# Two layers of linear attention and gated MLP on one core: nine zero products ahead of the first turn, first loads on either queue, turns in transpose mode, a new split of the last tile and a new order

## The chip, the cores and the metric

The kernel runs on one core of a Trainium2 chip. The metric is device time in microseconds (us) of one execution. Five engines matter: PE (TensorE, matrix products), DVE (VectorE), ACT (ScalarE), POOL (GpSimd) and SP (SyncE, which here does nothing but issue transfers). PE loads weights in parallel with products (PEld). Transfers are issued by SP, and a few by ACT, and run on 16 DMA engines.

## The reference

The input x is 2048 rows of 512 in bf16. Two layers run one after the other, each made of an attention block A and an MLP block B, with the same weights in both layers:

```python
q, k, v = split(layernorm(x) @ wqkv)          # 32 heads of 16
phi(u) = [softmax(u @ w_phi), softmax(-u @ w_phi)]   # per head, 16 + 16 wide
kv = phi(k).T @ v ;  z = sum over rows of phi(k)     # per head, over all 2048 rows
x = x + ((phi(q) @ kv) / (phi(q) @ z + 1e-6)) @ wo
n = layernorm(x)
x = x + ((relu(n @ W_gate) * (n @ W_up)) @ W_down)   # 1376 wide inside
```

The sums kv and z run over all rows. So no row of a layer's attention output can be made before the keys and values of all rows of that layer are done.

## The kernel before

The 2048 rows are 16 tiles of 128. A tile passes these steps in a layer, each a numbered operation ("op") of one engine:

- normalise (L479 to L506): row statistics on DVE (`stats` L481, 0.60 us, and `aggr` L482), `ln` and `rstd` on ACT (L489, L491), scaling on DVE (`xnA` L499).
- turn: the normalised 128x512 tile is transposed, as the products need the 512 on the partitions. Most tiles go by a DMA transpose on SP's queue, two tiles at a time (L465). The first four tiles of layer 0, the last two of layer 1's keys, and a few tiles in the MLP and in front of `wo` are turned by PE: four products with an identity matrix into a PSUM bank of 512 fp32 columns (L470), then a copy to SBUF (`evac`, L428 to L432) on ACT or DVE.
- keys and values: `K` (L539) and `V` (L545), each four products of 512 columns. ACT takes exp of the key product with both signs (`ek`, two of 512 columns), DVE sums over 16 (`sk` L550), ACT makes the reciprocal (`lnk`, `rk`), POOL or DVE scales (`phi` L513, two halves a tile), and PE adds the tile to the sums (`kvz` L574, eight products of 65 columns).
- queries: `Q` (L601), exp (`Eq`), sum (`sq` L607), scaling (`rat`, `phq` on POOL or DVE), then a DMA transpose (`fq` L627).
- When all 16 `kvz` are done, DVE writes the summed matrix into `R` (L586). Then `erq` (L638), division, `o`, turn, `proj` with `wo` (L661), residual, and the MLP: `G` and `Up` (L738), ReLU and product, `down` (L778), residual (`resB` L785). The MLP goes in blocks of 1 to 4 tiles.

The key and query weights are folded with w_phi at the start: the key weight `wk` is turned by PE (`turn` L444, four ops m = 0 to 3 of four products), copied (`wT`), multiplied by a block-diagonal `Wblk` (`fold` L452, ops 0 to 3), and copied to `Wk` (`W2`). `K` of any tile needs all four `W2`. The query weight takes the same way with DMA transposes (`wT` L439) and folds 4 to 7. Below, fold 4 to 7 and W2 4 to 7 are those of the query weight.

Which engine does an op and when is written down by hand-over tables. `PLACE` is a string of 0 and 1, one for each op that two engines can do; 1 takes the other engine. `SLOTS` gives each buffer its place in its pool. `ORDER` lists all 1880 ops in one sequence; each engine executes its own ops in that sequence, in order, and waits at an op until its inputs are there. So a wait on an engine holds all that stands behind it. `IDLE` puts so many products with a zero matrix ahead of the n-th PE op; before the first one PE does eight of them (L425), which only keep PE busy.

Transfers take turns on eight completion semaphores: a load waits in its queue until the load eight places earlier has landed. First loads before: ACT issues `x` of tile 0 and half of `wk` (row blocks 2 and 3 of four, "wk2"); SP issues `wf`, the other half ("wk0", which turns 0 and 1 read; turns 2 and 3 read wk2), `x` of tiles 1, 2, 3, 4-5, 12-13, and then the first DMA transpose of the query weight.

Of the kernel before, what the change touches and what calls it, by code (L numbers as in the profile page):

```python
# [8 lines left out]
P = 128  # L9
D = 512  # L10
# [3 lines left out]
NB = D // P  # L14
# [128 lines left out]
class K:  # L143
# [9 lines left out]
    "0101010100000000001100000001110000101110000110101000000100000101000000010000100000011000000011101010"  # L153
    "1010011010111000101011000001100011100001011100000101101000111000000011000111010011000001101100001011"
    "0110101011100110011100010111110101000100110000001000001100000111100100010000110001001001011010111001"
    "010000101101110101001101111111110"
)
SLOTS = (
    "0011432021055021001401501045313321124221352412451013e0315g31303b0305c12201i012432332391030654220f321"
    "4h220030344d100111082247052a331k1615010b1250052c1344300g0132252j045e363d1200040401141402000224011020"  # L160
    "0400001134021012100000203101002122001002541105001002511102104910002413114215400412511651100100120031"
    "1420302310051535031h432112311505010425412301310405420324310022031410j5100a24022k02327101200410401103"
    "12242250121002352020511310154521505223522020e4231c031213111011021411125513140225000g3420030030020120"
    "03413125121121433231f0121f214i00181651332422193104055j333k204b360a2243033d242h304i113805010401021210"
    "0000121002100010010021140010123402000043001010020111302020011511301002431321101003205504010521311411"
    "5402110501523540013000121032150140030110232043213110025124210401311015522400200403422412313320414041"
    "210100300531330452512524210005215103213300111020141500412"
)
IDLE = (
    0, 0, 0, 1, 0, 0, 0, 0, 0, 0, 1, 0, 1, 0,  # L170
# [101 lines left out]
)  # L272


# [620 lines left out]
```

## Time and profile before

| what | value |
|---|---|
| median of 3 runs | 375.89 us (375.27 to 376.62) |
| the profiled execution | 376.44 us, of which the span (first to last instruction) 374.7 us |
| PE busy in the span | 363.8 us (97%) |
| DVE, ACT, POOL busy | 275.9, 204.3, 80.4 us |
| first product of `K` | 10.18 us |
| first `erq` (all keys of layer 0 summed) | 56.30 us |
| last product starts / last store has landed | 371.22 / 373.71 us |

A row of the groups reads: line, engine, operation, output<-inputs, shape and count, then busy time and mean duration, then the idle time of the engine ahead of these instructions and what ended it. A row of the stages reads: stretch, length, then busy us and count of PE, PEld, DVE, ACT and POOL, the granted clock, the DMA share and GB/s. Durations are longer than what an instruction holds its engine, as neighbours overlap; where the text counts a queue it takes the distance from start to start of neighbours without a wait: 0.863 us for four products of 512 columns, 0.26 for `kvz`, 0.223 for four of 128 columns, 0.477 for an ACT exp of 512, 0.465 for an ACT copy of 512, 1.129 for `sk` and `sq`, 0.60 for `stats`, 0.602 for `phi` on DVE, 1.014 on POOL, 0.60 for a DVE copy of 512 out of PSUM, 0.335 for a DVE product of 512 bf16 from SBUF.

### The profile page before, as it was taken

What the parts mean: (1) busy time and instruction counts of PE and PEld (TensorE: products, weight loads), DVE (VectorE), ACT (ScalarE), POOL (GpSimd) and SP (SyncE); (2) the same over time, 40 slices, a digit from 0 to 9 for tenths busy, and PEclk for the clock granted to TensorE, in tenths of its full rate; (3) what the DMA queues carried; (4) which work ended last, traced back from release to release, by engine and by line L of the source; (5) the groups of instructions that cost most, each with busy time, mean ns of one, the idle gap of its engine ahead of it and who ended that gap; (6) DMA issues with size and microseconds to landing.
All of it is one profiled execution on the core that took longest, in us unless ns stands there. A gap on an engine that the chain in (4) does not pass through costs nothing.

```text
span 374.7 us, 7403 instructions
## 1 busy us (share of the span) xinstructions
PE 363.8 (97%) x2784; PEld 216.1 (58%) x2830; DVE 275.9 (74%) x587; ACT 204.3 (55%) x561; POOL 80.4 (21%) x93
## 2 busy tenths in 40 slices
PE   7998999999999999999999999999999999999996
PEld 3453455867544544466566456587764444457674
DVE  6999999998775956864789989998776365134333
ACT  5998999655545546344539666874434423313111
POOL 0286985430101100110033533241100000000000
PEclk9999999999999999999999999999999999999999
DMA  8997439875532233042212100488753302020221
GB/s 233 204 232 195 131 81 175 142 142 112 96 59 54 44 65 63 1 84 52 42 38 48 36 0 3 85 115 121 147 94 79 57 0 58 0 56 2 69 74 42
DMA packets 93443, 31.20 MB, mean 83 GB/s; under 512 B 85248, under 2 KB 92384, under 8 KB 93408
## 3 DMA queue, kind: packets, MB, share of 16 engines
q1 hardware_dynamic: 92992, 30.34, 40.1%
q8 instruction: 22, 0.36, 0.4%
q10 hardware_dynamic: 416, 0.39, 0.4%
q14 instruction: 13, 0.11, 0.1%
HBM read 7.91 MB, written 2.10 MB: 27 GB/s over the span
## 4 chain that ended last, share of the span: by engine, by line
PE 89%; issue 1%; ACT 0%; DVE 0%; DVEq 0%
PE b L738 37%; PE b L778 20%; PE b L661 7%; PE b L601 6%; PE b L545 6%; PE b L539 5%; PE b L714 3%; PE q L638 2%; PE q L574 2%; PE b L470 1%; ACT ek L604 0%; DVE o L652 0%; DVE X L785 0%; DVEq L890 0%; ACT lnA L489 0%
## 5 line engine op out<-in xcount | busy, mean ns | idle before, releaser
L738 PE MATMUL b<-xnTB,wgu 128*128 128x128 bf16 (+2 forms) x1200 | 154.5, 279 | 0.2 <-ACT rd L649 0.2
L738 PEld LDWEIGHTS <-wgu 128*128 128x128 bf16 x1200 | 97.5, 98 | 47.3 <-DMA xnTB<-xn 0.4
L742 ACT ACTIVATE gu<-b 128x512 bf16<-128x512 f32 (+1 forms) x83 | 47.2, 581 | 84.8 <-PE b L738 82.0
L778 PE MATMUL b<-wd,hT 128*128 128x512 bf16 (+2 forms) x342 | 83.9, 372 | 0.9
L513 POOL TENSOR_TENSOR ek<-ek,sk 128x512 bf16<-128x512 bf16 x43 | 46.7, 1107 | 122.6 <-ACT sk L562 121.7
L778 PEld LDWEIGHTS <-hT 128*128 128x128 bf16 (+1 forms) x363 | 34.7, 98 | 34.2 <-DVE hT L746 0.2
L755 DVE TENSOR_TENSOR hT<-gu,b 128x512 bf16<-128x512 bf16 (+1 forms) x47 | 30.8, 666 | 30.2 <-ACT gu L742 16.4
L607 DVE TENSOR_REDUCE sq<-ek 128x64 f32<-128x1024 bf16 x32 | 38.4, 1210 | 3.6 <-ACT ek L604 3.5
L604 ACT ACTIVATE ek<-b 128x512 bf16<-128x512 f32 x64 | 37.0, 606 | 6.9 <-PE b L601 6.7
L542 ACT ACTIVATE ek<-b 128x512 bf16<-128x512 f32 x64 | 36.8, 623 | 6.6 <-PE b L539 6.6
L550 DVE TENSOR_REDUCE sk<-ek 128x64 f32<-128x1024 bf16 x32 | 38.2, 1205 | 1.8 <-ACT ek L542 1.8
L785 DVE SCALAR_TENSOR_TENSOR X<-b,rsB,X 128x512 bf16<-128x512 f32 (+1 forms) x33 | 23.9, 729 | 21.2 <-PE b L778 21.0
L757 ACT CAST gu<-b 128x512 bf16<-128x512 f32 (+1 forms) x36 | 20.5, 569 | 25.9 <-PE b L738 25.7
L539 PE MATMUL b<-Wk,xnTA 128*128 128x512 bf16 x122 | 32.2, 379 | 1.1 <-DMA xnTA<-xn 0.6
L545 PE MATMUL b<-wv,xnTA 128*128 128x512 bf16 x124 | 31.8, 379 | 1.3 <-ACT ek L604 1.0
L661 PE MATMUL b<-wo,oT 128*128 128x512 bf16 x121 | 31.5, 379 | 0.4
L622 POOL TENSOR_TENSOR ek<-ek,sq 128x512 bf16<-128x512 bf16 x24 | 25.3, 1060 | 30.4 <-DVE rsB L701 14.3
L601 PE MATMUL b<-Wq,xnTA 128*128 128x512 bf16 x121 | 30.8, 379 | 0.4
L665 DVE SCALAR_TENSOR_TENSOR X<-b,X 128x512 bf16<-128x512 f32 x32 | 22.0, 686 | 9.8 <-PE b L661 9.4
L652 DVE TENSOR_TENSOR o<-q,rd 128x512 bf16<-128x512 f32 x32 | 22.0, 687 | 2.8 <-PE b L738 1.2
L481 DVE BATCH_NORM_STATS2 bstA<-X 128x6 f32<-128x512 bf16 x32 | 21.1, 681 | 2.0 <-DMA X<-in_A_x_dram 1.8
L746 DVE TENSOR_TENSOR hT<-gu 128x512 bf16<-128x512 bf16 (+1 forms) x36 | 15.2, 424 | 10.1 <-ACT gu L757 10.0
(74 smaller groups left out, 351.0 us busy)
## 6 DMA issues: line engine op xcount, KB each, us to landing
out_dram<-X SPq DMA_DIRECT2D x15, 128.0 KB, 1.8
X<-in_A_x_dram SPq DMA_DIRECT2D x6, 256.0 KB, 4.5
wgu<-in_B_W_up_dram SPq DMA_DIRECT2D x4, 344.0 KB, 3.5
wgu<-in_B_W_gate_dram SPq DMA_DIRECT2D x4, 344.0 KB, 4.7
wd<-in_B_W_down_dram SPq DMA_DIRECT2D x5, 256.0 KB, 3.4
wv<-in_A_wqkv_dram SPq DMA_DIRECT2D x2, 256.0 KB, 4.4
wo<-in_A_wo_dram SPq DMA_DIRECT2D x4, 128.0 KB, 3.5
fq<-ek SPq DMA_TRANSPOSE x32, 3.3
```

Source lines behind the costliest of these rows:

```text
L513: e.tensor_tensor(out=out().rearrange("p g s (h f) -> p (g s h) f", f=DH)[:, lo:lo + n], in0=ek.t[:].rearrange("p g s (h f) -> p (g s h) f ...
L539: k = op("PE", mm(4, 512), due, lambda: [nc.tensor.matmul(kp.t[:], lhsT=xnTA[c][:, i, b, :], rhs=Wk2[:, b, :], start=(b == 0), stop=(b == ...
L542: e = [op("ACT", act(512), due, lambda s=s: nc.scalar.activation(out=ek.t[:, :, s, :], in_=kp.t[:].rearrange("p (g e) -> p g e", e=GQ), fu ...
L545: v = op("PE", mm(4, 512), due_v, lambda: [nc.tensor.matmul(vp.t[:], lhsT=xnTA[c][:, i, b, :], rhs=wv[:, b, :], start=(b == 0), stop=(b == ...
L550: a = op("DVE", SUM16, due, lambda: nc.vector.tensor_reduce(out=sk.t[:, row, :], in_=ek.t[:].rearrange("p g s (h f) -> p (g s h) f", f=DH) ...
L601: q = op("PE", mm(4, 512), due, lambda: [nc.tensor.matmul(qp.t[:], lhsT=xnTA[c][:, i, b, :], rhs=Wq2[:, b, :], start=(b == 0), stop=(b == ...
L604: e = [op("ACT", act(512), due, lambda s=s: nc.scalar.activation(out=ek.t[:, :, s, :], in_=qp.t[:].rearrange("p (g e) -> p g e", e=GQ), fu ...
L607: a = op("DVE", SUM16, due, lambda: nc.vector.tensor_reduce(out=sq.t[:], in_=ek.t[:].rearrange("p g s (h f) -> p (g s h) f", f=DH), axis=A ...
L661: a = op("PE", mm(4, 512), due + 3, lambda j=j, yp=yp: [nc.tensor.matmul(yp.t[:], lhsT=oT.t[:, j, b, :], rhs=wo[:, b, :], start=(b == 0), ...
L738: nc.tensor.matmul(ps.t[:, q * W:(q + 1) * W].rearrange("p (i t) -> p i t", t=P), lhsT=wgu[:, s, b, g * P:(g + 1) * P], rhs=xT.t[:, 0:n, b ...
L742: nc.scalar.activation(out=gu.t[:, 0, 0:cols], in_=gp.t[:, 0:cols], func=AF.Relu)
L778: nc.tensor.matmul(yp.t[:, 0:c1 - c0], lhsT=h.t[:m, f * W + i * P:f * W + (i + 1) * P], rhs=wd[:m, f, c0:c1], start=(f == 0), stop=(f == N ...
```

## The change

- The op ahead of the first turn makes nine zero products instead of eight. `IDLE` holds two products ahead of fold 4, instead of one each ahead of fold 0, fold 4 and the first `K`.
- The loads of `x` of tiles 0 and 1 and of the two halves of `wk` can be issued by SP or ACT, and `PLACE` has four more digits for them. They begin 1, 1, 0, 1: `x` of tile 0 and wk2 move to SP, `x` of tile 1 moves to ACT. So ACT issues one of these loads, and SP three.
- PE turns (`turn`, and the four-product turns of `xnTA`, `xnTB`, `oT`) use transpose mode. The result stands in bf16 in the first half of the PSUM bank, and the copies read bf16. The arrangement tables count a DVE copy of it at double rate.
- The last tile of layer 1 makes its output columns as 384 and 128 instead of 256 and 256.
- `ORDER`, `SLOTS` and `PLACE` are new throughout. PE's work is the same ops.

The diff without the tables:

```diff
-    op("PE", mm(8, 512), 0, lambda: idle(8), [c_z], [wps], name="warm")
+    op("PE", (3630, 3800, 9), 0, lambda: idle(9), [c_z], [wps], name="warm")
...
-    def load(due, dst, src, nbytes, eng="SP", follow=()):
-        q = nc.sync if eng == "SP" else nc.scalar
-        return op(eng, dma(nbytes), due, lambda: q.dma_start(out=dst, in_=src), name="load", follow=follow,
-                  move=nbytes / RATE)
+    def load(due, dst, src, nbytes, eng="SP", follow=(), both=False):
+        queues = {"SP": nc.sync, "ACT": nc.scalar}
+        ways = {e: (e, dma(nbytes), lambda q=q: q.dma_start(out=dst, in_=src), False) for e, q in queues.items()}
+        return op(eng, dma(nbytes), due, ways[eng][2], name="load", follow=follow, move=nbytes / RATE,
+                  alt=ways["ACT" if eng == "SP" else "SP"] if both else None)
...
+    def half(ps):
+        return ps.t[:].bitcast(BF16)[:, 0:NB * P]
...
-            tr = op("PE", mm(4, 128), due + m, lambda m=m, ps=ps: [nc.tensor.matmul(
-                ps.t[:, b * P:(b + 1) * P], lhsT=w[:, m, b * P:(b + 1) * P], rhs=ident[:], start=True, stop=True)
+            tr = op("PE", mm(4, 128), due + m, lambda m=m, ps=ps: [nc.tensor.transpose(
+                half(ps)[:, b * P:(b + 1) * P], w[:, m, b * P:(b + 1) * P], ident[:]) for b in range(NB)], ...
...
-            halves = ((0, 256), (256, 512)) if l == 1 and t == T - 1 else ((0, 512),)
+            halves = ((0, 384), (384, 512)) if l == 1 and t == T - 1 else ((0, 512),)
...
 IDLE = (
-    0, 0, 0, 1, 0, 0, 0, 0, 0, 0, 1, 0, 1, 0,
+    0, 0, 0, 0, 0, 0, 0, 0, 0, 0, 0, 2, 0,
 )
```

The tables read out by engine, for the first ops (numbers behind a name are tiles; `turn`, `fold`, `wT` and `W2` carry their own numbers; x12 stands for tiles 12-13, and so on):

| engine | before | after |
|---|---|---|
| SP | wf, wk0, x1, x2, x3, x4, x12, query turn 0, wv2, x8, wv0, x14, query turn 2, x6, query turn 1, wo, turn of tiles 4-5, W_down, turn of 12-13, W_down, x10, W_down, query turn 3, W_up, W_down, wo, W_gate, turn of 8-9 | wk0, x0, wf, wk2, x3, x12, x4, query turn 0, x2, wv2, wv0, query turn 3, x8, query turn 2, W_up, turn of 4-5, x6, query turn 1, x14, wo, W_down, turn of 8-9, wo, x10, turn of 12-13 |
| ACT | x0, table, wk2, ln and rstd 0, wT 0 and 1, ln 1, W2 0, rstd 1, wT 3, wT 2, copy of tile 0's turn, W2 1, 3, 2 | x1, table, ln and rstd 1, ln 0, wT 0 and 1, rstd 0, wT 2, W2 0, 1, 2, 3, copy of tile 1's turn |
| DVE | constants, masks, zero, stats 0, Wblk, stats 1, xnA 0, stats 2, 3, xnA 1 | zero, constants, masks, stats 1, stats 0, Mg, Wblk, xnA 1, xnA 0, wT 3, stats 3, copy of tile 0's turn |
| PE | 8 zero products, turns 0, 1, (1) fold 0, turns 3, 2, turn of tile 0, folds 1, 3, 2, (1) fold 4, turn of tile 1, (1) K0, K1 | 9 zero products, turns 0 to 3, folds 0, 1, turn of tile 1, fold 2, turn of tile 0, fold 3, (2) fold 4, K0, K1 |

Over the whole kernel `phi` on DVE goes from 21 to 15 (POOL 43 to 49), `phq` on DVE from 8 to 5, `vext` copies on DVE from 7 to 4, `ssq` on DVE from 11 to 15, the direct MLP product on DVE from 47 to 44, and six tiles turned by PE are copied by DVE instead of one, besides wT 3. Ahead of the first `R` DVE's queue loses one `sq`, one `vext` copy and one `phq`, and gains the copies wT 3 and of the turns of tiles 0 and 2, and one `rat`.

More of the change, by code (lines that the diff above doesn't have):

```diff
@@ L361, in w_load @@
     def w_load(w, k, b, eng):
-        return lambda f: load(b, w[:, b:b + 2, :], wqkv[:, b:b + 2, k * D:(k + 1) * D], 262144, eng, f)
+        return lambda f: load(b, w[:, b:b + 2, :], wqkv[:, b:b + 2, k * D:(k + 1) * D], 262144, eng, f, w is wk)
     def first_x(t, n, eng="SP"):
@@ L423, in idle, with evac @@
             nc.tensor.matmul(wps.t[:, 0:NB, :], lhsT=zero[:, 0:P], rhs=zero[:], start=True, stop=True)
-    op("PE", mm(8, 512), 0, lambda: idle(8), [c_z], [wps], name="warm")
-    def evac(eng, due, out_, in_, deps, takes, uses, name, cols=512):
+    op("PE", (3630, 3800, 9), 0, lambda: idle(9), [c_z], [wps], name="warm")
+    def evac(eng, due, out_, in_, deps, takes, uses, name, cols=512, rate=1):
         both = {"ACT": ("ACT", act(cols), lambda: nc.scalar.copy(out=out_(), in_=in_()), False),
-                "DVE": ("DVE", dve(cols), lambda: nc.vector.tensor_copy(out=out_(), in_=in_()), False)}
+                "DVE": ("DVE", dve(cols, rate), lambda: nc.vector.tensor_copy(out=out_(), in_=in_()), False)}
         _, cost, copy, _ = both[eng]
         return op(eng, cost, due, copy, deps, takes, uses, name=name, alt=both["DVE" if eng == "ACT" else "ACT"])
+    def half(ps):
+        return ps.t[:].bitcast(BF16)[:, 0:NB * P]
     def fold(w, dst, loaded, due, step, engs, by_dma=False):
@@ L443, in fold @@
             ps = Buf(p_b)
-            tr = op("PE", mm(4, 128), due + m, lambda m=m, ps=ps: [nc.tensor.matmul(
-                ps.t[:, b * P:(b + 1) * P], lhsT=w[:, m, b * P:(b + 1) * P], rhs=ident[:], start=True, stop=True)
-                for b in range(NB)], [loaded[m * len(loaded) // NB], c_id], [ps] + ([wT] if m == 0 else []),
+            tr = op("PE", mm(4, 128), due + m, lambda m=m, ps=ps: [nc.tensor.transpose(
+                half(ps)[:, b * P:(b + 1) * P], w[:, m, b * P:(b + 1) * P], ident[:]) for b in range(NB)], [loaded[m * len(loaded) // NB], c_id], [ps] + ([wT] if m == 0 else []),
                 [] if m == 0 else [wT], name="turn")
             turned.append(evac(engs[m % 2], due + m, lambda m=m: wT.t[:, :, m * P:(m + 1) * P],
-                               lambda ps=ps: ps.t[:].rearrange("p (b d) -> p b d", d=P), [tr], (), [ps, wT], "wT"))
+                               lambda ps=ps: half(ps).rearrange("p (b d) -> p b d", d=P), [tr], (), [ps, wT], "wT",
+                               rate=2))
         for m in range(NB):
@@ L469, in turn @@
         ps = Buf(p_b)
-        a = op("PE", mm(NB, 128), due, lambda: [nc.tensor.matmul(
-            ps.t[:, b * P:(b + 1) * P], lhsT=src.t[:, 0, b * P:(b + 1) * P], rhs=ident[:], start=True, stop=True)
-            for b in range(NB)], after + [c_id], [ps], [src], name=name)
-        return evac("ACT", due, lambda: dst()[:, 0], lambda: ps.t[:].rearrange("p (b t) -> p b t", b=NB), [a],
-                    takes, [ps] + uses, name, 512)
+        a = op("PE", mm(NB, 128), due, lambda: [nc.tensor.transpose(
+            half(ps)[:, b * P:(b + 1) * P], src.t[:, 0, b * P:(b + 1) * P], ident[:]) for b in range(NB)], after + [c_id], [ps], [src], name=name)
+        return evac("ACT", due, lambda: dst()[:, 0], lambda: half(ps).rearrange("p (b t) -> p b t", b=NB), [a],
+                    takes, [ps] + uses, name, 512, 2)
     def nothing():
```

28 lines of the change are left out of this document (14 added, 14 removed), and 180 rows, old and new, of the table ORDER.

## The prediction

> **What bounds the kernel now.** I read the totals and the chain that ended last first, then the stages, then PE's waits, then the timeline of the start and SP's queue.
>
> ```profile
> PE 363.8 (97%) x2784; PEld 216.1 (58%) x2830; DVE 275.9 (74%) x587; ACT 204.3 (55%) x561; POOL 80.4 (21%) x93
> ...
> PE 89%; issue 1%; ACT 0%; DVE 0%; DVEq 0%
> ```
>
> PE is busy 97% of the span, and the chain is PE's. The change leaves PE's products as they are (the turns keep their number and their 128 columns, 11 zero products stay 11), so time can only be won where PE waits: 374.7 - 363.8 = 10.9 us. The stages tell where.
>
> ```profile
> 0.00:40.00 40.00, 35.12 (x233) 17.55 (x238) 36.51 (x78) 33.40 (x96) 18.78 (x24) 1.00 0.88 208
> 40.00:80.00 40.00, 39.31 (x432) 25.62 (x437) 39.08 (x65) 34.46 (x109) 26.53 (x32) 1.00 0.66 135
> 80.00:120.00 40.00, 39.56 (x285) 23.95 (x288) 29.56 (x78) 21.17 (x60) 2.18 (x3) 1.00 0.50 92
> ...
> 360.00:374.70 14.70, 11.44 (x134) 8.78 (x131) 5.30 (x9) 1.95 (x4) 0.00 (x0) 1.00 0.16 49
> 20.00:40.00 20.00, 18.28 (x130) 9.11 (x131) 20.00 (x32) 17.82 (x53) 15.47 (x16) 1.00 0.85 207
> 40.00:56.00 16.00, 15.84 (x141) 8.65 (x143) 16.00 (x18) 15.72 (x48) 14.91 (x16) 1.00 0.40 109
> ```
>
> 4.9 us lie in the first 40, 3.3 in the last stage (the store and the end), and 2.7 in all between. The second thing to see is DVE's column: 20.00 of 20 and 16.00 of 16 up to the first `erq` at 56.30. There DVE has no hole at all, while PE has 1.7 + 0.2.
>
> ```profile
> PE q L423 <- DVE zero L394: 2.0, 1, 2.0
> PE b L545 <- ACT ek L604: 1.0, 1, 1.0
> PE b L452 <- ACT hT L429: 0.7, 2, 0.4
> PE b L539 <- DMA xnTA<-xn: 0.6, 1, 0.6
> PE b L539 <- ACT Wk L429: 0.2, 1, 0.2
> ```
>
> These are PE's waits of the first 40 us. The order of the start:
>
> ```profile
> 0.83 0.07 DVE L396 MEMSET vext<- 128x8 bf16 x1 [0.83 <-PEq L879]
> 1.63 0.27 DVE L394 MEMSET zero<- 128x256 uint32 x1
> 1.96 3.59 PE L423 MATMUL q<-zero 128*128 128x512 bf16 x8 [1.96 <-DVE zero L394]
> 5.57 0.82 PE L444 MATMUL b<-ident,hT 128*128 128x128 bf16 x8
> 6.20 1.07 ACT L429 CAST hT<-b 128x512 bf16<-128x512 f32 x2 [1.74 <-PE b L444]
> 9.35 1.61 ACT L429 CAST Wk<-b 128x512 bf16<-128x512 f32 x3
> 11.01 1.71 PE L539 MATMUL b<-Wk,xnTA 128*128 128x512 bf16 x6 [0.24 <-ACT Wk L429]
> ```
>
> From 6.20 on ACT copies without a hole; its last `Wk` copy ends at 10.96 and K0's third product starts at 11.01. PE's rate changes on the way: zero products start 0.427 apart, the turns 0.107 until 6.06, then 0.056, and later 512 columns take 0.216. The granted clock shows 1.00 in all these stages, so the step has to be read from the spacing; it came 4.1 us after PE's first product.
>
> **The change, part by part.**
>
> *Zero products.* `zero` becomes DVE's first op: 0.83 + 0.27 = 1.10, and PE follows 0.06 later as before, at 1.16. Nine at 0.427 end at 5.00. Before, eight ended at 5.34 and the first turn waited until 5.57 for wk0, which landed at 5.52.
>
> *First loads.* wk0 goes first on SP (0.74 instead of 1.25); with its old 4.28 it lands at 5.0, with fewer bytes ahead perhaps at 4. Turn 0 thus starts at 5.0, 0.57 earlier. wk2 becomes SP's fourth load. The five loads x0, x1, wf, wk0 and wk2 had all landed at 5.83 before, and are now the first five again, so I take 5.83 (bounds 5.3, as before, and 6.2, one tile's load later). The first query turn has 128 KB less ahead, so 8.57 or earlier. ACT's part falls from two issues to one (0.47).
>
> *ACT to K0.* Its first copy came 0.63 after the first turn's start: 5.63. Then wT 0, 1 (0.477 each), one `rstd` (0.10), wT 2, W2 0 to 3: seven copies, the last from 8.6 to 9.2. Before, ACT had wT 3, the copy of tile 0's turn, and two more small ops in this row, so 10.96 becomes 9.2. Wait of the inputs: turn 3 ends about 6.7 if PE is still slow, `fold` 0 by 6.95, W2 0 starts 7.16: hidden. wT 3 and tile 0's copy now wait in DVE's queue, which reaches them at 7.0 and 8.0, ahead of need. K0 ends about 9.5 instead of 11.4, and K1, behind ACT's copy for tile 1, starts at 9.75 instead of 11.68: PE is 1.9 us ahead.
>
> *What is late next: DVE.* PE's queue from K0 to the first `erq` holds 44 x 0.863 + 16 x 0.26 + 5 x 0.223 = 43.2 us in both orders. Before, 10.18 + 43.2 = 53.4 became 56.30, so 2.9 was lost on the way. With no wait at all it would now be about 8.6 + 43.2 = 51.8 (K0's end less its own 0.86). But `erq` needs `R`, and DVE's queue ahead of `R` shrinks only by `sq` 1.129 + `vext` 0.601 + `phq` 0.602, and grows by three copies and one `rat` 0.10. No row shows a DVE copy of bf16 out of PSUM; the nearest are 0.60 (fp32 PSUM) and 0.335 (bf16 SBUF). I take 0.335, since the source has the same type, and keep 0.60: -1.23, or -0.43. DVE also starts ahead: `stats` 1 at 3.0 (x1, as x0 before) and `stats` 0 at 4.3 fill what was a hole of 0.87 before 5.86; with Mg (0.31) done early I count 0.5 (0.2 to 0.9). Together 1.7 (0.6 to 2.1). PE would then stand 1.1 to 2.8 us ahead of DVE and wait for `R`, so DVE's 1.7 is what reaches the first `erq`: 54.6.
>
> ACT's queue ahead of `R` loses three copies and one `lnq`/`rq` pair and gains one `vext` and one `Eq`: -0.7, plus the 0.57 earlier start, -1.3, and it had 2.2 us of holes in 20 to 40. POOL keeps 26 `phi` and loses a `rat` and a `phq`. Neither sets it.
>
> *SP's queue.* The turn of tiles 8-9 stood behind W_up, W_down, wo and W_gate and took 5.88 where others took 3.07:
>
> ```profile
> 23.37 1.23 SPq L465 DMA_TRANSPOSE xnTA<-xn  x1
> 29.30 1.04 PE L539 MATMUL b<-Wk,xnTA 128*128 128x512 bf16 x4 [0.57 <-DMA xnTA<-xn]
> ```
>
> Now it stands behind x6, x14, wo and W_down, and DVE has its input ready after 15.3 us of queue instead of 17.0, so about 19.2. Landing at 22.3 to 25, PE wants it (K9, 13.4 us of queue after K0's start) at 22.
>
> *Zero products in `IDLE`.* Three of 0.216 become two, ahead of `fold` 4, while the query turn or W2 3 is awaited: 0. If neither is, 0.43 at most.
>
> *Transpose mode.* 72 products of 128 columns at 0.056: no row shows the mode, I take the same, 0. ACT copies of bf16 out of PSUM: 0.465, as for fp32, since the SBUF row for 512 bf16 (0.520) is not shorter.
>
> *Rest.* From `erq` 0 to the 17th tile's keys DVE's queue changes by only -0.2, so its lead is kept; behind 80 us DVE has room (29.6 of 40) and PE sets the pace with the same products. New waits there: 0, between -0.7 (a quarter of the 2.7) and +0.7.
>
> *Last tile.* The same columns, 22 products. The 384-column residual occupies DVE 0.40 + 0.13; the last one, 128 wide, starts 0.34 after PE's end instead of 0.27 but takes 0.34 instead of 0.475. With half the bytes in the last store: -0.1 (0 to -0.2).
>
> **Sum.** 376.44 - 1.7 - 0.1 = 374.6 for an execution like the profiled one, which stands 0.55 over the median; against the median 375.89 it is **374.1 us**.
>
> **Rivals.**
>
> *The clock steps up late.* The step came 4.1 us after the first product, and the turns then were ordinary products. If turns in transpose mode do not count as work, the count begins anew with the folds at 6.4 and ends at 10.5: 0.4 longer to the last W2 and 0.8 on K0 and K1. For: PE would do zero products only until 5.00. Against: from 1.16 to 5.00 it works without a hole, and step + 4.1 is 5.3. PE's lead over DVE pays most of the 1.2, so 374.6, at worst 375.3. The Trainium skill (TensorE: Matmul & The Clock Gate, "Part 4: PE-mode transpose") says just this: transposes don't count as PE-busy for the clock gate. By that rule the step comes late and the sum is 374.6; the trace of before, which has no transposes, can't show it.
>
> *Turns behind bulk loads.* The turn of 6-7 now follows W_up and W_down, 600 KB; if it, or that of 8-9, again needs 5.88 instead of 3.07, `K` is 2.8 late, DVE runs dry behind it, and the 1.7 is gone: 375.8. For: the row above. Against: the loads are spread wider.
>
> *Slower: the second join.* Before the second layer's `R`, tile 14's two `phi` halves, one of which DVE did, now both stand on POOL behind one of tile 15's (2 x 1.014 in a row) ahead of the last `kvz`. From tile 14's normalised input on, one `sk` 1.13, the copy of the turn 0.335, five more DVE ops 3.5, its own `sk` 1.13, ACT 0.77, POOL 2.03, `kvz` 0.26, `R` 0.7 and some 0.6 of hand-overs add to 10.5 us; PE has 11 x 0.863 + 11 x 0.26 = 12.4 of queue to cover it. Once DVE is over 1.9 late there, PE waits for each further us; over 3.7 late, the kernel is slower than before. Against: PE waited only 0.4 in 200 to 240, and DVE was busy 37.9 of the 40. At the 5 us that would decide it beyond doubt, 374.1 + 3.1 = 377.2.
>
> *Faster: PE's waits vanish.* If DVE turns out to have kept pace with PE (its rows were lengthened by waits that no view shows), the 54.6 becomes nearer 53: 372.5.
>
> **How the numbers follow.** Forecast 0.47, late clock 0.15, bulk loads 0.20, second join 0.08, waits vanish 0.10. 0.3% of 375.89 is 1.13 us, about what a measurement can tell: faster means below 374.76, slower above 377.0. Faster: 0.45 of the forecast, 0.08 of the late clock, and 0.10: 0.63. Slower: 0.08 of the join and 0.01 of the bulk loads: 0.09. Same: 0.28. The forecast's own range is 373.2 to 375.0 (DVE's 0.6 to 2.1, rest 0.7). The range overall runs from 372.7 to 376.2, leaving out the far half of the vanished waits and the join.
>
> **What would show it.** First zero product near 1.16, first turn near 5.0, spacing 0.056 by turn 2; last `Wk` copy's end near 9.2; K1 near 9.75; DVE again without a hole from 6 to the first `R`, `erq` near 54.6 with a wait of PE for `R` or for `sk`'s followers in front of it. I am wrong if K0 stays behind 10.5 (loads or clock), if DVE shows holes while `K` waits for a transpose, or if the lead at the first `erq` is lost again before 240 us.

## The result

The changed kernel takes 373.62 us (373.38 to 374.11) against 375.98 us (375.27 to 376.62) for the kernel before, run beside it: a ratio of 0.9925, 95% interval 0.9911 to 0.9939, so 0.6 to 0.9% faster: 2.4 us by the medians, 2.8 by the ratio. That is more than the 0.3% that can be told from no change. The forecast was 374.1, its own range 373.2 to 375.0. Run once more (e5 below) the same kernel came to 0.9927 (0.9911 to 0.9943). The profiled execution took 373.38 us, its span is 371.5.

Totals and chain of the changed kernel:

```profile
PE 366.2 (99%) x2830; PEld 216.0 (58%) x2830; DVE 271.0 (73%) x587; ACT 203.5 (55%) x553; POOL 87.4 (24%) x104
...
PE 84%; ACT 6%; DVE 2%; DMA 1%; issue 0%; DVEq 0%
```

PE is idle for 5.3 us now. One caution: this trace holds all 2830 products, that of before 2784, so the 366.2 against 363.8 us of busy time are in part the records missing there. Starts of named instructions, used from here on, don't suffer from that.

The stages, columns as before (length, then busy us and count of PE, PEld, DVE, ACT and POOL, granted clock, DMA share, GB/s):

```profile
0.00:40.00 40.00, 38.28 (x258) 19.41 (x259) 36.28 (x80) 35.65 (x100) 20.51 (x26) 1.00 0.84 200
40.00:80.00 40.00, 39.61 (x446) 26.82 (x445) 38.17 (x70) 34.25 (x108) 22.01 (x28) 1.00 0.68 140
...
360.00:371.50 11.50, 8.33 (x96) 5.98 (x92) 4.01 (x8) 1.84 (x4) 0.00 (x0) 1.00 0.26 82
20.00:40.00 20.00, 19.89 (x133) 9.64 (x132) 20.00 (x33) 19.63 (x59) 17.74 (x18) 1.00 0.81 183
40.00:53.20 13.20, 13.15 (x122) 7.05 (x121) 12.87 (x17) 12.90 (x41) 10.35 (x11) 1.00 0.42 131
```

From 20 us to the first `R` all of DVE, ACT and PE are now full: PE 19.89 of 20 where it had 18.28. DVE is full in both kernels. So a full DVE column in the stage from 20 to 40 didn't tell that DVE did the same amount of useful work in it; that is where the size of the gain went wrong, as will be seen.

PE's waits in the first 60 us, and the start in order of time:

```profile
PE q L424 <- DVE zero L395: 1.2, 1, 1.2
PE b L448 <- DMA hT<-in_A_wqkv_dram: 0.4, 1, 0.4
PE b L474 <- ACT ek L607: 0.2, 1, 0.2
```

```profile
0.86 0.27 DVE L395 MEMSET zero<- 128x256 uint32 x1 [0.86 <-PEq L882]
1.19 4.02 PE L424 MATMUL q<-zero 128*128 128x512 bf16 x9 [1.19 <-DVE zero L395]
3.99 0.69 DVE L484 BATCH_NORM_STATS2 bstA<-X 128x6 f32<-128x512 bf16 x1 [2.36 <-DMA X<-in_A_x_dram]
5.00 1.06 PE L448 MATMUL b<-ident,hT 128*128 128x128 bf16 x8
6.42 0.70 PE L448 MATMUL b<-ident,hT 128*128 128x128 bf16 x8 [0.35 <-DMA hT<-in_A_wqkv_dram]
7.45 2.07 ACT L430 CAST Wk<-b 128x512 bf16<-128x512 f32 x4
8.96 2.13 PE L542 MATMUL b<-Wk,xnTA 128*128 128x512 bf16 x8
```

The waits of 1.0 for `ek` and 0.6 for a transposed tile are gone. A wait for the second piece of Wk at 6.42 is new.

Four marks divide the two profiled executions:

| mark | before | after | difference |
|---|---|---|---|
| first product of `K` | 10.18 | 8.96 | -1.22 |
| first `erq` | 56.30 | 53.29 | -3.01 |
| last product starts | 371.22 | 368.11 | -3.11 |
| end of the span | 374.65 | 371.50 | -3.15 |

Everything is won ahead of the first `erq`; from there to the last product it is 314.9 and 314.8 us. The two profiles differ by 3.06 us in time where the medians differ by 2.36: that of before stood 0.46 above its median of 375.98, that of after 0.24 below.

Behind `K`'s first product, PE has the same work up to the first `erq` in both kernels. In the profile after, which misses no record, the distances from start to start less the waits add to 43.24 us, the 43.2 of the prediction. So 53.29 = 8.96 + 43.24 + 1.09 of waits, and before 56.30 = 10.18 + 43.24 + 2.89. Seen from PE, the change won 1.22 at the head and 1.80 of waits. Seen from DVE, whose queue runs into the same `R`, the same 3 us look like this (time that each group of operations holds the queue, up to `R`'s end):

| on DVE up to the first `R` | before | after | difference |
|---|---|---|---|
| normalisation `xn` (x16) | 7.55 | 5.36 | -2.19 |
| `sq`, `vext`, `phq` less the three copies and one `rat` | | | -1.24 |
| everything else | | | -0.15 |
| idle | 2.66 | 3.20 | +0.54 |
| sum | | | -3.04 |

Of the 0.54 more idle, 0.21 is a wait for `x` of tiles 6-7 at 17.80 and 0.32 a wait for the last `kvz` ahead of `R`; without these two DVE idles 2.67 against 2.66.

The largest row is sixteen operations that the change left alone in number and size. In the groups by line (busy, mean ns, then idle before) they read as follows, the kernel before first, then the changed one:

```profile
L499 DVE TENSOR_SCALAR xn<-X,mvA,rsA 128x512 bf16<-128x512 bf16 x16 | 8.5, 554 | 0.4 <-ACT rsA L491 0.4
```

```profile
L502 DVE TENSOR_SCALAR xn<-X,mvA,rsA 128x512 bf16<-128x512 bf16 x16 | 6.5, 428 | 0.1
```

Most take 0.38 to 0.41 us; three of before took 1.13 to 1.16. The timelines of DVE and POOL in the kernel before show two of these:

```profile
26.84 2.21 DVE L499 TENSOR_SCALAR xn<-X,mvA,rsA 128x512 bf16<-128x512 bf16 x2
...
26.78 2.12 POOL L513 TENSOR_TENSOR ek<-ek,sk 128x512 bf16<-128x512 bf16 x2 [0.74 <-ACT sk L562]
```

POOL begins two `phi` multiplications at 26.78, DVE two normalisations at 26.84, and both pairs end together, at 28.9 and 29.05, although DVE alone needs 0.7 for its pair. The same holds for every long row: over the 14 profiles of before, after and the runs below, every `xn` row over 0.48 us, 50 in all, began while POOL multiplied and ended 0.15 us after that multiplication, and no row that began while POOL stood idle took more than 0.42. After the change such pairs fall into POOL's pauses (DVE first, POOL second):

```profile
22.18 0.70 DVE L502 TENSOR_SCALAR xn<-X,mvA,rsA 128x512 bf16<-128x512 bf16 x2
25.72 0.73 DVE L502 TENSOR_SCALAR xn<-X,mvA,rsA 128x512 bf16<-128x512 bf16 x2
...
22.81 3.08 POOL L516 TENSOR_TENSOR ek<-ek,sk 128x512 bf16<-128x512 bf16 x3 [0.52 <-ACT sk L565]
26.39 4.16 POOL L516 TENSOR_TENSOR ek<-ek,sk 128x512 bf16<-128x512 bf16 x4 [0.50 <-ACT sk L565]
```

POOL stops at 22.29 and at 25.89, DVE's pairs run from 22.18 to 22.88 and from 25.72 to 26.45. DVE shows as busy while it is held, so no view of idle time and no view of waits tells of it: only the duration of single rows against the others of their group does.

### The profile page after: what moved, and what is told of

It reads as the page before. It is cut to its first block, busy times and chain, and to the rows that moved or that the text cites. A ratio compares the mean times of both kernels' runs of the same rounds, so it can differ in the third digit from the quotient of the medians.

```text
span 371.5 us, 7439 instructions
## 1 busy us (share of the span) xinstructions
PE 366.2 (99%) x2830; PEld 216.0 (58%) x2830; DVE 271.0 (73%) x587; ACT 203.5 (55%) x553; POOL 87.4 (24%) x104
## 4 chain that ended last, share of the span: by engine, by line
PE 84%; ACT 6%; DVE 2%; DMA 1%; issue 0%; DVEq 0%
PE b L741 38%; PE b L781 20%; PE b L664 7%; PE b L604 5%; PE b L548 4%; PE b L542 4%; PE b L717 3%; ACT ek L545 3%; PE q L641 2%; ACT ek L607 2%; PE q L577 1%; DMA xnTB<-xn 1%; DVE ek L516 1%; ACT vext L430 1%; PE b L474 1%; ACT sk L565 0%
## 5 line engine op out<-in xcount | busy, mean ns | idle before, releaser
L741 PE MATMUL b<-xnTB,wgu 128*128 128x128 bf16 (+2 forms) x1200 | 152.3, 280 | 0.1
L781 PE MATMUL b<-wd,hT 128*128 128x512 bf16 (+3 forms) x363 | 86.1, 373 | 0.0
L516 POOL TENSOR_TENSOR ek<-ek,sk 128x512 bf16<-128x512 bf16 x49 | 52.5, 1095 | 69.1 <-ACT sk L565 49.2
L758 DVE TENSOR_TENSOR hT<-gu,b 128x512 bf16<-128x512 bf16 (+1 forms) x44 | 28.9, 663 | 32.9 <-ACT gu L745 17.3
L788 DVE SCALAR_TENSOR_TENSOR X<-b,rsB,X 128x512 bf16<-128x512 f32 (+2 forms) x33 | 23.9, 731 | 20.5 <-PE b L781 20.4
L604 PE MATMUL b<-Wq,xnTA 128*128 128x512 bf16 x128 | 32.0, 379 | 0.0
L625 POOL TENSOR_TENSOR ek<-ek,sq 128x512 bf16<-128x512 bf16 x27 | 28.4, 1057 | 8.4 <-DVE sq L621 6.4
L621 POOL TENSOR_TENSOR sq<-sq 128x32 f32<-128x32 f32 x22 | 6.6, 300 | 90.8 <-ACT sq L617 71.4
L760 ACT CAST gu<-b 128x512 bf16<-128x512 f32 (+1 forms) x39 | 21.8, 565 | 8.2 <-PE b L741 8.2
L749 DVE TENSOR_TENSOR hT<-gu 128x512 bf16<-128x512 bf16 (+1 forms) x39 | 17.2, 444 | 11.0 <-ACT gu L760 11.0
```

The source lines that it names most:

```text
L516: e.tensor_tensor(out=out().rearrange("p g s (h f) -> p (g s h) f", f=DH)[:, lo:lo + n], in0=ek.t[:].rearrange("p g s (h f) -> p (g s h) f ...
L604: q = op("PE", mm(4, 512), due, lambda: [nc.tensor.matmul(qp.t[:], lhsT=xnTA[c][:, i, b, :], rhs=Wq2[:, b, :], start=(b == 0), stop=(b == ...
L741: nc.tensor.matmul(ps.t[:, q * W:(q + 1) * W].rearrange("p (i t) -> p i t", t=P), lhsT=wgu[:, s, b, g * P:(g + 1) * P], rhs=xT.t[:, 0:n, b ...
L781: nc.tensor.matmul(yp.t[:, 0:c1 - c0], lhsT=h.t[:m, f * W + i * P:f * W + (i + 1) * P], rhs=wd[:m, f, c0:c1], start=(f == 0), stop=(f == N ...
```

## The experiments

Theory after the result: DVE's queue sets the first `R`, and in the kernel before 2.2 us of it were normalisations held by POOL. Rivals: the gain is that of the shorter start (PE's path), or that of the turns' mode. All four times below the marks come from the profile of each run, the ratio from its times beside the kernel before on the same chip. "Waits" is what PE loses from `K`'s first product to the first `erq`, counted from start to start: the difference of these two less 43.24. (The idle time that the views show is less, as the ends of products are modelled.)

| run | `K` first | waits | first `erq` | ratio to before (95%) |
|---|---|---|---|---|
| before (profile) | 10.18 | 2.89 | 56.30 | 1 |
| after (profile) | 8.96 | 1.09 | 53.29 | 0.9925 (0.9911 to 0.9939) |
| e5, after again | 9.43 | 1.27 | 53.94 | 0.9927 (0.9911 to 0.9943) |
| e1, before, two `xn` moved | 9.76 | 1.42 | 54.42 | 0.9972 (0.9957 to 0.9987) |
| e2, after, two `xn` moved back into POOL's work | 8.85 | 3.54 | 55.63 | 0.9974 (0.9961 to 0.9987) |
| e3, after, DVE +1.13 us | 9.43 | 2.80 | 55.48 | 0.9961 (0.9949 to 0.9973) |
| e4, after, PE +1.08 us | 8.98 | 1.13 + 1.08 | 54.43 | 0.9936 (0.9918 to 0.9954) |
| e6, after, ordinary turns | 9.09 | 1.50 | 53.83 | 0.9970 (0.9955 to 0.9984) |
| e7, after, x0 loaded first | 8.80 | 1.18 | 53.21 | 0.9931 (0.9916 to 0.9947) |
| e8, after, zero turns | 8.94 | 0.88 | 53.07 | 0.9953 (0.9936 to 0.9970) |
| e9, before, turns in transpose mode | 10.09 | 2.15 | 55.48 | 0.9994 (0.9978 to 1.0009) |
| e10, after, wk2 by ScalarE | 9.33 | 1.31 | 53.88 | 0.9936 (0.9915 to 0.9957) |
| e11, after, one `phi` to POOL | 9.12 | 1.33 | 53.69 | 0.9948 (0.9933 to 0.9964) |
| e12, after, e10 and e11 | 9.52 | 1.72 | 54.48 | 0.9962 (0.9948 to 0.9975) |

One execution of one kernel differs from another by some 0.65 us at the first `erq` (after and e5), so single marks closer than that decide nothing. DVE's rows show where this comes from. The new order issues `x` of tiles 6-7 behind the turn of tiles 4-5 on SP, and DVE waits for it, first in the changed kernel and then in e4:

```profile
17.80 0.69 DVE L484 BATCH_NORM_STATS2 bstA<-X 128x6 f32<-128x512 bf16 x1 [0.21 <-DMA X<-in_A_x_dram]
18.93 0.69 DVE L484 BATCH_NORM_STATS2 bstA<-X 128x6 f32<-128x512 bf16 x1 [1.44 <-DMA X<-in_A_x_dram]
```

From the start of this row to the first `erq` it is 35.5 us in after, e4, e5, e6, e7 and e10 alike (35.49 to 35.51); the row starts at 17.80, 18.93, 18.44, 18.33, 17.71 and 18.37. So in this order DVE's queue sets the first `R` from that row on, and what is won or lost ahead of it is taken up by the wait, as far as the wait reaches. The kernel before has no such wait. Why the load landed between 17.02 (e8, no wait) and 18.90 (e4) stays open.

**Held normalisations.** e1 takes the kernel before and moves one op of its order: `stats` of tile 15 (285) behind the two normalisations of tiles 6 and 7 (157, 158), which then start before POOL does. e2 does the reverse to the changed kernel: `xn` of tile 14 (289) goes ahead of `stats` 11 (219), and `xn` of tile 10 (223) behind `vext` 9 (210). Each edit moves one number or two of `ORDER`:

```diff
 e1 (kernel before), in ORDER:
-    285, ..., 157, ..., 158,
+    ..., 157, ..., 158, 285,
 e2 (changed kernel), in ORDER:
-    219, ..., 289,          223, ..., 210,
+    289, 219, ...,          ..., 210, 223,
```

> The kernel before, with DVE's two xnA of tiles 6 and 7 moved ahead of one stats op, so that they fall into POOL's pause at 26.0 to 26.8. Theory (DVE's queue sets the first R, and an xnA that meets a running POOL phi waits for its end): the two rows shrink from 1.15 us to 0.4, first erq at 54.8 instead of 56.3, time lower by 1.5 us (374.5). Rival (PE's late start sets it): the rows may shrink, erq stays at 56.3, time within 0.3 us of before.

> The changed kernel, with two xnA put into running POOL phi ops: the first xnA of tiles 14-15 ahead of one stats op, the first of tiles 10-11 behind a vext copy. Theory: each takes 1.1 us instead of 0.4 or 0.6, DVE's queue ahead of R grows by 1.2 to 1.4 us, first erq at 54.6 instead of 53.3, time 374.9. Rival (PE's queue sets it): erq and time as in the changed kernel, 373.6.

The rows of DVE in e1:

```profile
20.14 1.13 DVE L499 TENSOR_SCALAR xn<-X,mvA,rsA 128x512 bf16<-128x512 bf16 x1
25.84 0.71 DVE L499 TENSOR_SCALAR xn<-X,mvA,rsA 128x512 bf16<-128x512 bf16 x2
```

The pair takes 0.71 instead of 2.21; the third long one, at 20.14, was left where it was. The waits fall from 2.89 to 1.42, and the kernel before gets 0.28% (0.13 to 0.43) faster by one moved op: 1.1 us, where the changed kernel's ratio is worth 2.8. In e2 (DVE's rows, then POOL's):

```profile
28.10 0.86 DVE L502 TENSOR_SCALAR xn<-X,mvA,rsA 128x512 bf16<-128x512 bf16 x1
33.44 0.91 DVE L502 TENSOR_SCALAR xn<-X,mvA,rsA 128x512 bf16<-128x512 bf16 x1
36.53 1.18 DVE L502 TENSOR_SCALAR xn<-X,mvA,rsA 128x512 bf16<-128x512 bf16 x1
...
26.75 4.14 POOL L516 TENSOR_TENSOR ek<-ek,sk 128x512 bf16<-128x512 bf16 x4 [0.51 <-ACT sk L565]
32.13 3.13 POOL L516 TENSOR_TENSOR ek<-ek,sk 128x512 bf16<-128x512 bf16 x3 [1.24 <-ACT sk L565]
35.49 5.16 POOL L516 TENSOR_TENSOR ek<-ek,sk 128x512 bf16<-128x512 bf16 x5 [0.22 <-ACT sk L565]
```

Three rows of 0.86 to 1.18 stand inside POOL's work, PE's waits rise to 3.54, and of the changed kernel's 0.73% only 0.26% is left. The first `erq` came 2.34 us later, not 1.2 to 1.4 as expected: the `xn` rows make 1.34, a `phi` of DVE's at 48.89 that was held too makes 0.48, and `x` of tiles 6-7 makes 0.34. `K` starts as early in e2 as in the changed kernel (8.85), so the shorter start is worth little when DVE is late: this speaks against the first rival. The Trainium skill (SBUF — State Buffer, "SBUF: two separate sides") states that VectorE and GpSimd share one pair of ports; of a GpSimd operation and a VectorE operation of the kinds that use the pair, the one that starts first keeps it for its whole length while the other waits. The rows agree in both directions; e11 below shows the other one, there with a run of DVE's operations. The prediction did not draw on that rule.

**Work added to one queue.** e3 makes the sum of tile 5's keys twice on DVE, e4 has five more zero products on PE at 15.98 us, ahead of a fold of the query weight:

```diff
 e3
-                ... axis=AX.X, op=Alu.add),
+                ... axis=AX.X, op=Alu.add)
+                for _ in range(2 if (self.l, t) == (0, 5) else 1)],
 e4
-    0, 0, 0, 0, 0, 0, 0, 0, 0, 0, 0, 2, 0,
+    0, 0, 0, 0, 0, 0, 0, 0, 0, 0, 0, 2, 0, 0, 0, 0, 0, 0, 0, 0, 0, 0, 5,
```

> The changed kernel, with DVE's sum sk of tile 5 in layer 0 made twice: 1.13 us more in DVE's queue. Theory: DVE has no slack ahead of R, so first erq at 54.4 and time +1.1 (374.7). Rival: PE's queue sets R, DVE has slack, time +0.3 at most.

> The changed kernel, with five more zero products of 512 columns (5 x 0.216 = 1.08 us) in PE's queue between the keys of tiles 5 and 2 of layer 0. Theory: PE stands ahead of DVE, so part of it is hidden: time +0.0 to +0.5. Rival (PE's queue sets the first erq): +1.1 us (374.7).

e3 is slower than the changed kernel by 0.34% of 376.7, 1.3 us: the whole 1.13 of DVE's work arrives, and more, since everything behind it shifts and one `xn` falls into POOL's work (1.14 us at 27.65). From its wait for `x` of tiles 6-7 to the first `erq` it is 37.3 us instead of 35.5. e4's profile has the first `erq` 1.14 later (54.43), but that says nothing of PE: in this execution `x` of tiles 6-7, issued at 13.83 and so ahead of the added products, landed at 18.90 instead of 17.77, DVE waited 1.44 for it, and the 35.5 us from there are those of the changed kernel. The profiled execution is also the longest of e4's seven (375.15). Its time is 0.35 us above the changed kernel's by the ratio (0.9936 against 0.9927, with intervals of 0.0016 to 0.0018 on either side), and 1.1 by the medians (374.76 against 373.64 in e5, beside kernels before of 376.69 and 376.72). That DVE's queue sets the first `R` is shown by e2 and e3. Whether PE's queue is level with it is not settled: e4 leaves room for a slack between nothing and about 1 us.

**The turns' mode.** e6 gives the changed kernel ordinary products for its turns (float32 PSUM, order and places unchanged). e9 gives the kernel before turns in transpose mode and nothing else.

```diff
 e6
-            tr = ... [nc.tensor.transpose(half(ps)[:, b * P:(b + 1) * P], w[:, m, b * P:(b + 1) * P], ident[:])
+            tr = ... [nc.tensor.matmul(ps.t[:, b * P:(b + 1) * P], lhsT=w[:, m, b * P:(b + 1) * P], rhs=ident[:], ...)
 e9 (kernel before): the reverse
```

> The changed kernel with its turns as ordinary products into fp32 PSUM, order and places unchanged. Theory (VectorE's queue sets the first R): the three copies of turned blocks that VectorE makes before the first R take about 0.60 us each instead of 0.33, so the first product that needs R (53.29 us) comes 0.8 us later, at 54.1, and the kernel takes about 374.4. ScalarE's copies change too but are not on that path. Rival (the turns' mode delays the clock and that costs time): the step to the full rate comes earlier than 6.6 us, K's products start before 8.96 us, and the kernel takes 373.0 to 373.6, no longer than the changed one.

> The kernel before, in its own order, with its turns in transpose mode and nothing else of the change. Ahead of the first R the kernel before has all copies of turned blocks on ScalarE, and a ScalarE copy of 512 columns takes 0.58 us from float32 and from bf16 alike. Theory (the mode pays only where VectorE makes the copies, 0.33 us instead of 0.60): nothing changes ahead of the first R, so the time stays within 0.2% of the kernel before, ratio 0.998 to 1.002, and K's first products stay at 9.8 to 10.2 us. Rival (the mode itself brings part of the gain, by faster turns or faster ScalarE copies): 0.5 us or more sooner, ratio 0.9985 or below with the first product that needs R at 55.7 us or sooner.

DVE's copies of turned x over the whole kernel, in the changed kernel and in e6 (busy, mean ns):

```profile
L431 DVE COPY xnTA<-b 128x512 bf16<-128x512 bf16 x3 | 1.2, 407 | 0.0
L431 DVE COPY xnTB<-b 128x512 bf16<-128x512 bf16 x2 | 0.8, 411 | 0.0
```

```profile
L431 DVE CAST xnTA<-b 128x512 bf16<-128x512 f32 x3 | 2.0, 674 | 0.0
L431 DVE CAST xnTB<-b 128x512 bf16<-128x512 f32 x2 | 1.4, 677 | 0.0
```

From start to start that is 0.33 for a copy of bf16 and 0.59 to 0.60 for one of float32; the three ahead of the first `R` add 0.80. e6 is 0.43% slower than e5 on the same chip, 1.6 us, twice as much as expected. Its first `erq` hardly moves in the profile (53.83, e5 53.94): the three copies start at 7.2, 8.4 and 14.8, ahead of the wait for `x` of tiles 6-7, and DVE still waits 0.37 there. So in this profile the path that the expectation named cost nothing. From there to the last product it takes 316.2 us, the changed kernel 314.8. That is lost on DVE behind the second `R`, first e6 and then the changed kernel:

```profile
237.05 0.69 DVE L431 CAST oT<-b 128x512 bf16<-128x512 f32 x1
237.65 1.19 DVE L684 TENSOR_SCALAR xn<-X,rowsum 128x512 bf16<-128x512 bf16 x1
...
240.49 0.67 DVE L431 CAST xnTB<-b 128x512 bf16<-128x512 f32 x1
```

```profile
236.43 0.42 DVE L431 COPY oT<-b 128x512 bf16<-128x512 bf16 x1
236.76 0.44 DVE L684 TENSOR_SCALAR xn<-X,rowsum 128x512 bf16<-128x512 bf16 x1
...
238.85 0.41 DVE L431 COPY xnTB<-b 128x512 bf16<-128x512 bf16 x1
```

Ahead of these rows e6 is 0.62 behind the changed kernel. The copy of `oT` adds 0.27, the normalisation 0.74, the copy of `xnTB` 0.27: 1.28 of DVE's queue, and PE, which has no wait here in the changed kernel, waits for `xnTB`. The normalisation is again a held one: POOL multiplies from 236.63 to 238.70, and this row ends at 238.84. It came 0.27 later into POOL's work than its counterpart in the changed kernel. In e9, where DVE makes no such copy ahead of the first `R`, the mode gives 0.06% (-0.09 to 0.22): nothing. So the mode is not worth anything by itself; it pays because the changed order lets DVE make the copies, and there it decides between 0.3% and 0.73%.

e9's first `erq` is at 55.48 all the same, 0.82 sooner than before, and DVE's pair of normalisations shows why:

```profile
26.76 1.45 DVE L500 TENSOR_SCALAR xn<-X,mvA,rsA 128x512 bf16<-128x512 bf16 x2
```

The first of the pair began 0.08 ahead of POOL's multiplication (26.84), took 0.39, and only the second was held (1.14). Two of the three rows are held here, and PE's waits are 0.74 less; so in the order of before the number of held rows seems to vary from execution to execution.

**The clock.** e5 repeats the changed kernel. e8 replaces the nine zero products of 512 columns by 36 zero turns in transpose mode, so that PE does nothing but transposes until its first fold.

```diff
 e8
-            nc.tensor.matmul(wps.t[:, 0:NB, :], lhsT=zero[:, 0:P], rhs=zero[:], start=True, stop=True)
+            nc.tensor.transpose(wps.t[:, 0, :].bitcast(BF16)[:, 0:P], zero[:, 0:P], ident[:])
```

> The changed kernel again, as the measure for the three runs beside it: 0.992 to 0.994 of the kernel before. What it shows beside that: whether the step of TensorE's rate from 107 ns a turn to the full rate, which came 5.5 us after the first zero product in the profiled execution, comes at the same place again. If turns in transpose mode do not count as work for the clock (the rival called late clock), it should come at 6 to 7 us each time; if it varies for other reasons, it may come anywhere from 4 to 7 us.

> The changed kernel with its nine zero products of 512 columns replaced by 36 zero turns in transpose mode of 128 columns. If turns in transpose mode do not count for the clock, TensorE has then no counted work before K's first products: the rate stays at 107 ns for 128 columns past 9 us, K's first products of 512 columns take about 0.43 us each, and K0 comes at 9.5 us or later. If they count as ordinary products do, the step comes 3 to 5.5 us after the first of them, at 4 to 7 us, as with zero products. The time: VectorE sets the first R, so 373.5 to 374.5 in either case; above 374.5 would show that a late clock reaches the end.

The start of PE in e8:

```profile
1.36 4.00 PE L424 MATMUL q<-ident,zero 128*128 128x128 bf16 x36 [1.36 <-POOL ident masks.py:199]
5.15 1.06 PE L448 MATMUL b<-ident,hT 128*128 128x128 bf16 x8
6.42 0.62 PE L448 MATMUL b<-ident,hT 128*128 128x128 bf16 x8 [0.22 <-DMA hT<-in_A_wqkv_dram]
```

Eight turns take 1.06 us at 5.15 (starts 0.107 apart) and 0.62 at 6.42 (0.056 apart): the full rate is there 5.1 us after the first transpose, with no other product before it. The Trainium skill's statement (TensorE: Matmul & The Clock Gate, "Part 4: PE-mode transpose") that transposes don't count for the gate, which the prediction weighed, does not hold here; the run decides. Whether the step would come without any work on PE no run shows. Over all profiles the step came 2.9 us (e2, e6) to 6.0 us (e11) after PE's first product, and in the changed kernel itself at 6.65 and at 5.3 us, so the rival called late clock could not be told from chance by one profile. The Trainium skill (TensorE: Matmul & The Clock Gate, "Part 1: The HAM clock gate") describes a window of 3.4 us that runs on its own, whatever the kernel does; a spread of 3.1 us among the runs agrees with that, though not with the 0.5 us either way that the section gives for the step. Late steps show no cost: e11's first `K` came at 9.12 with the step at 7.2, e6's at 9.09 with the step at 4.1, since ACT's copies of `Wk` stand between.

e8's time is 0.26% above that of e5, although its first `erq` came at 53.07. Its median of 374.60 lies just over the 374.5 that was to show a late clock reaching the end, but the step was not late here, so the bound shows nothing. Behind it, PE waited 0.5 us for a transposed `oT` at 244.7 and later for an `xnTB`, which the changed kernel's profile doesn't show. Why these transfers came late there stays open.

**Attempts to win more.** Two loads and one multiplication:

```diff
 e7, in ORDER: x of tile 0 ahead of the first piece of Wk on SP; rstd 0 ahead of wT 0 on ACT
-    3, ..., 0, ...            48, ..., 31, ..., 49
+    0, 3, ...                 48, 49, ..., 31
 e10, in PLACE: the second piece of Wk by ACT
-    "11010100...
+    "10010100...
 e11, in PLACE and ORDER: phi 20 (tile 10) on POOL
 e12: e10 and e11
```

> The changed kernel with the load of x's tile 0 ahead of the first piece of Wk on SP's queue, and rstd of tile 0 ahead of the first copy of turned weights on ScalarE. Theory: VectorE's first statistics, which waited until 3.99 us for x, start at about 3.0 us; VectorE is busy from there to the first R, so that comes 0.5 to 1.0 us sooner and the kernel takes 372.6 to 373.1. Rival (the weights' path sets the start): the first piece of Wk lands 0.6 to 1 us later, the turns and K's first products (8.96 us) come later by that, VectorE then waits for the first scores what it won at the start, and the time stays at 373.4 to 374.

> The changed kernel with one load moved back: the second piece of Wk goes through ScalarE's queue, behind x's tile 1, instead of being fourth on SP's. TensorE has waited for that piece for 0.35 to 1.1 us in each profile of the changed kernel and its variants, at 6.4 to 6.9 us. Up to the first product that needs R TensorE has 43.24 us of work behind K's first product, and in the changed kernel only 1.1 us of waits among it. Theory (TensorE's queue now sets that point as much as VectorE's): the wait falls to 0.3 us or less, K's first product comes 0.3 to 0.6 us sooner, at 8.4 to 8.7 us, of which VectorE's queue lets a part through: 373.2 to 373.6. Rival (VectorE alone sets it): K's first product comes sooner, the waits behind it grow by the same, and the time stays at 373.6 to 373.8. A third way: x's tiles land later beside it, VectorE starts later, and the time is 374 or more.

> The changed kernel with one multiplication of VectorE (0.59 us, the one of tile 10's that stands third from last ahead of R) moved to POOL, which is idle from 48.7 to 51.4 us. Theory (both queues are level at the first R): only TensorE's last two waits ahead of R, 0.21 and 0.18 us at 51.7 and 52.9, can go, so the first product that needs R comes 0.2 to 0.4 us sooner and the kernel takes 373.2 to 373.4. Rival (VectorE alone sets it): 0.6 us sooner, 373.0. Other rival (POOL's operation is not ready in time, or holds VectorE's neighbours as the others did): 374 or more, with a long row on VectorE between 48 and 52 us or a wait of TensorE for POOL.

> The two edits of the two runs before together. If TensorE's and VectorE's queues are level at the first R, a gain needs both to become shorter, and the two together bring more than the sum of each alone: the first product that needs R at 52.5 to 52.9 us, 372.7 to 373.2. If VectorE alone sets it, this is as the run with the multiplication on POOL; if TensorE alone, as the run with the load on ScalarE's queue.

None beats the changed kernel. e7's DVE starts at 3.52 (3.74 in e5), `K` at 8.80, the first `erq` at 53.21, and its time is that of e5 within the intervals: whether a few tenths are won isn't shown. The 0.5 to 1.0 us expected did not come: DVE waited 0.46 for `x` of tiles 6-7, which landed at 17.69, so an earlier start alone could win nothing. Issuing that load sooner was not tried. In e10 the wait for Wk went, and another took its place:

```profile
PE b L456 <- DVE Wblk L412: 0.7, 1, 0.7
PE b L542 <- DMA xnTA<-xn: 0.4, 1, 0.4
```

DVE waited 0.88 for x of tile 0 (its statistics begin at 5.16, in e5 at 4.7), `Wblk` stands behind these, and `K` begins at 9.33, no sooner. The third way of its expectation holds, though the time is only 0.09% up. In e11, DVE's row and POOL's:

```profile
48.93 2.48 DVE L516 TENSOR_TENSOR ek<-ek,sk 128x512 bf16<-128x512 bf16 x4
...
49.54 2.79 POOL L516 TENSOR_TENSOR ek<-ek,sk 128x512 bf16<-128x512 bf16 x1 [0.75 <-ACT sk L565]
```

POOL's operation, 1.06 us long elsewhere, takes 2.79: it ends 0.9 after DVE's four multiplications in a row. Here it is POOL that is held. PE then waits 0.36 for it, and the other rival of e11's expectation holds (374.26 us). POOL's idle time beside a DVE that multiplies is not free time. e12 has both new waits, and is slower than either.

## Why the prediction was right, and where it was not

**Which queue decides: right.** The prediction put the gain down to DVE's queue ahead of the first `R`, with nothing behind it. e3 (1.13 us more on DVE cost 1.3) and e2 bear it out, and from the first `erq` to the last product both profiles have 314.8 to 314.9 us. What it didn't have is that the new order lets DVE's queue start anew at 17.80, when `x` of tiles 6-7 has landed.

**DVE's operations: right.** Worked out as -1.23, measured -1.24, with the copy of bf16 out of PSUM at 0.33 (taken 0.335, with 0.60 as the other bound). e6 shows that this choice carried more than the prediction had it carry: at 0.60 the cost was 1.6 us and not 0.8. In e6's profile none of it is lost at the first `R`, as the copies stand ahead of the wait for `x` of tiles 6-7; it is lost behind the second `R`, where DVE falls 1.28 behind and PE has less room than the rival of the second join gave it (1.9); the changed kernel has no wait there.

**The head start: not won.** Counted as 0.5 won on DVE, it brought nothing: up to the wait at 17.80 DVE idles as long as before (2.67 and 2.66), and the waits for `x` of tiles 6-7 and for the last `kvz` (0.53) came on top. x of tile 1 landed at 3.97, not 3.0, and DVE stood idle until 3.99; in the runs with the same loads it began between 3.41 (e8) and 3.75 (e3), never at 3.0. The step took `x0`'s landing of before (2.97) for x1 on the same queue with two 256 KB pieces beside it; the first pieces of Wk and x went ahead of each other differently from what the byte count said (wk0 at 4.18 instead of 5.0, wk2 at 6.37 instead of 5.83, outside its bounds of 5.3 to 6.2).

**Normalisations held by POOL: not in the sum, -2.19.** This is the term that sizes the result. The step read DVE's full columns (20.00 of 20, 16.00 of 16) as work, and so took only what the change adds and removes. The clause of the last rival, that rows were lengthened by waits that no view shows, was the right one, and its first `erq` "nearer 53" is the one measured. It got 0.10 because nothing was looked up behind it: the profile of before showed `xn` at 381 to 1155 ns in one group, and that spread would have told.

**The sum.** Predicted for DVE -1.7, measured -3.04 in the profiles (-1.24 - 2.19 - 0.15 + 0.54): the first `erq` at 53.29 instead of 54.6. Between two such executions 1.8 us were forecast and 3.06 came. That the predicted 374.1 lies only 0.5 above the median is in part luck: the largest term was missing, a term of 0.5 brought nothing, and the forecast starts from a median of three executions, 375.89, where 17 to 28 executions of the kernel before beside the experiments have medians of 376.53 to 376.72.

**The smaller steps.** First zero product 1.19 (1.16), turn 0 at 5.00 (5.0), the last `Wk` copy's end at 9.5 (9.2), `K` of tile 1 at 10.05 (9.75): the 0.3 is wk2's. The turn of tiles 8-9 was issued at 19.15 and landed at 23.08, within the bounds; 3.93 instead of 5.88, so the rival of the bulk loads fell, though in e4 a late load did leave DVE dry for 1.44 us. The tail: last product to end 3.44 before, 3.39 after, so 0.05 instead of 0.1; the split was not tried by itself. DVE was to have no hole from 6 us to the first `R`: it had 0.13 at 11.9, the 0.21 at 17.80 and the 0.32 ahead of `R`. PE was to wait for `R`, 1.1 to 2.8 ahead of DVE: it waited about 0.4 in front of it, 0.21 ahead of the last `kvz` and 0.18 ahead of the first `erq`, as DVE was faster than forecast.

**The late clock.** The step did come late in the profile of after, 5.5 us after the first product, but no later than chance makes it, and it cost nothing that can be seen.

## What to carry to other kernels

A column that is full says that an engine had no hole, not that it worked: before summing what a change adds and removes on it, look in each group for rows far above the minimum, and see what the engine that shares its way to SBUF was doing at that time. Where VectorE and GpSimd both work on SBUF, the order of the two decided here over more than the number of operations; moving one op past another was worth 1.1 us here, and moving work to an idle GpSimd nothing. A cheaper operation pays where the order puts it on the queue that binds: the same transposes were worth 1.6 us in one order and nothing in the other. And where a queue starts anew at a late load, time saved ahead of that load is not won: look for the last row that waits for a transfer before adding up a queue from its start.

## What was not expected of the hardware

- A DVE normalisation of 512 bf16 from SBUF (0.38 us) took up to 1.19 us where a POOL multiplication (1.06 us) had begun before it, and ended 0.15 us after it, 50 times of 50; a POOL multiplication took 2.79 us beside DVE's multiplications in a row. Reductions on DVE (1.2 us) show no such thing beside POOL's long runs.
- TensorE reached its full rate with nothing but transposes before the step (e8), 5.1 us after the first.
- The step to the full rate came 2.9 to 6.0 us after the first product, and differed by 1.3 us between two executions of one kernel, while the granted clock showed 1.00 throughout.
- A DVE copy of 512 bf16 out of PSUM holds its queue 0.33 us, of float32 0.60; on ACT both take 0.58.
